# Two weight tiles change places with a weight load, and side copies move behind the first outer products of each block

## The chip, the cores and the metric

The kernel runs on one core of one Trainium2 chip. The metric is device time in microseconds (us). Three executions of the kernel before took 599.28, 599.32 and 602.76 us; their median is 599.32 us. The profile is of another execution of the same kernel, which took 597.99 us; the span from its first to its last instruction is 596.2 us.

## What is computed

The reference is one decode step of a transformer block with conditioned layer norms, forward and backward in one launch:

```python
mod = (silu(c) @ w_mod).reshape(1, 6, 1, 1024)
sa, ca, ga, sb, cb, gb = mod[:, 0], ..., mod[:, 5]
h = layernorm(x) * (1 + ca) + sa
x = x + ga * attention(h, k_cache, v_cache, wq, wo)   # window of the last 4096 of 65536 keys
h = layernorm(x) * (1 + cb) + sb
x = x + gb * (((sigmoid(h @ w_gate)) * (h @ w_up)) @ w_down)
out, vjp = jax.vjp(f, x, k_cache, v_cache, wq, wo, w_gate, w_up, w_down, c, w_mod)
return out, *vjp(grad_out)
```

There is one token of width 1024, 32 query heads on 4 key heads of 128, and a hidden width of 3584. The outputs are the token and the gradients of all ten inputs. Each weight gradient is an outer product as large as the weight. The gradients of the two caches are zero outside the window, and these zeros (some 118 MB) have to be written as well.

## The kernel before, in words

One big tile in on-chip memory, `arena`, holds nearly everything. `ar(off, size)` cuts `size` KiB per partition from it at `off`, and the kernel reuses the same place for many things one after the other. The order of the instructions on each engine is written out by hand. Loads and stores are issued from two queues: POOL's (`nc.gpsimd`) carries most of them and all zero fills, SP's (`nc.sync`) carries the w_down traffic and some tiles of w_mod. Each queue issues in the order of the program: what waits at its head holds up all that stands behind it.

The zero fills are 1 MB writes which `zero(n)` takes from a list, some at each of many places (`Z_B`, `Z_FOLD`, `Z_FFN` and others hold how many).

The stretch around the change has two parts.

**The handover (about 284 to 312 us).** The attention part leaves eight tiles B_t[0] to B_t[7]. `bch` (L682) computes them in chunks on PE, and the last eight chunks, those of tile 7, run between the steps of `fold_half` (L871), which adds three sections of w_mod on PE and copies them back with ACT. The operands of the chunks of tile 7 stand in `ar(56, 8)`: two chunks are done with each 2 KiB of it, so places 56, 58, 60 and 62 come free in turn. The tiles `g_t` (L495) of the last section of w_mod are loaded into such places by `wm_sec` (L337). `mod_gb` (L610) reads them on PE and makes the vector gb, from which the broadcast row `b1k` is made (L933). B_t[4] and B_t[6] stand at 156 and 158, inside the second half of the w_down buffer `wd_v` (L846, places 152 to 160). So `load_wd(0, 1)` may be issued only when B_t[4] has been copied to `scr` and B_t[6] transposed by `tr_unit` (L833) into another home. `tr_unit` is eight PE transposes into one PSUM tile and one ACT copy out of it. After `rot[:] = [(psum, "mm")]` (L804) its PSUM tile, those of `fold_half` and those of `bcast` are one and the same bank.

**The block loop (about 320 to 475 us).** The hidden width is cut in seven blocks of 512. For block q the loop over j = 0 to 7 (L1022) runs on the tiles of w_up and w_gate (`ug_v`, two blocks' worth): DVE reduces the tile with the row `dug_b` (L1024), then the same place is overwritten by an outer product, the gradient, by ACT for j = 0 to 4 and by DVE for 5 to 7 (L1027). `store_ug` (L867) stores tiles 0 to 3 after j = 3 and the others after j = 7, `load_ug` (L863) refills the places for block q + 2. The next block then needs, in this order: `wd_ttr(q+1, 0)` on DVE (L977), `front` on PE (L948), `gates` on ACT (L959), `hh_ops` on DVE, `ffn_mm` on PE, `wd_ttr(q+1, 1)`, `dug_part` (PE and ACT, L986), and `wd_outer` (L981), which overwrites the w_down tile by its gradient and stores it on SP; `load_wd` for the block after waits for that store.

Beside this work runs a list of 45 side jobs (`jobs`, L935 and L996), each of them one `tr_unit`: transposes of tiles which the last part of the kernel needs. `side(n)` (L445) runs the next n of them at that place of the order. Their PSUM bank is also that of `dug_part`.

After the loop comes the last part: the gradients of the attention weights, the caches and w_mod, nearly all of it outer products and stores.

Of the kernel before, what the change touches and what calls it, by code (L numbers as in the profile page):

```python
# [58 lines left out]
def kernel(  # L59
# [26 lines left out]
    nc = tc.nc  # L86
# [13 lines left out]
    def ar(off, size):  # L100
        return arena[:, int(off * KIB):int((off + size) * KIB)]
# [51 lines left out]
    def zero(n, after=None):  # L153
        for _ in range(n):
            if len(zleft) <= keep[0]:
                return
            region, narrow_ = zleft.pop(0)
            first = None
            if narrow_:
                nc.gpsimd.inc_swdge_sem([], [], mode="reset_dge_cursor")  # L160
                n = nlen - ncount.pop()
                first = nc.gpsimd.dma_start(
                    out=rest[0:NS, 0:nlen * 128].rearrange("p (t x) -> p t x", t=2)[:, :, n * 64:(n + 1) * 64],
                    in_=zeros[0:NS, 0:64].rearrange("p (t x) -> p t x", t=1).broadcast_to([NS, 2, 64]))
                ins = nc.gpsimd.dma_start(
                    out=region[8:P, :].bitcast(FP32).rearrange("(t p) x -> p t x", t=2),
                    in_=zeros[0:60, :].rearrange("p (t x) -> p t x", t=1).broadcast_to([60, 2, ZW // 2]))
            else:
                ins = nc.gpsimd.dma_start(out=region.bitcast(FP32), in_=zeros[:, :])  # L169
            if after is not None:  # L170
                dep(first or ins, after)
# [16 lines left out]
    def new_tp(name="tp"):  # L188
        p, tag = next_pool()
        return p.tile([P, 1024], BF16, name=name, tag=tag)  # L190
# [7 lines left out]
    def addv(out, a, b):  # L198
        return tt(out, a, b, ALU.add)

    def cp(out, a):
        return nc.vector.tensor_copy(out=out, in_=a)  # L202
# [6 lines left out]
    def ttr(out, w, b, acc):  # L209
        return nc.vector.tensor_tensor_reduce(out=out, in0=w, in1=b, scale=1.0, scalar=0.0,  # L210
                                              op0=ALU.mult, op1=ALU.add, accum_out=acc)
# [117 lines left out]
    B_t = [junk if o is None else ar(o, 2) for o in B_off]  # L329
# [7 lines left out]
    def wm_sec(sct, j, n, off, eng=nc.gpsimd):  # L337
        eng.dma_start(out=ar(off, 2 * n).rearrange("p (j x) -> p j x", j=n),
                            in_=wm_view[:, j:j + n, sct * D:(sct + 1) * D])

    def mod_tiles(ps, tiles, ts_, first, last=KD - 1):
        for t in ts_:
            for k in range(KD):
                nc.tensor.matmul(ps[:, k:k + 1], lhsT=tiles[t][:, k * P:(k + 1) * P],
                                 rhs=cs_bf[:, t:t + 1], start=(first and t == ts_[0] and k == 0), stop=(t == last),
                                 skip_group_check=True)
# [98 lines left out]
    def side(n=1):  # L445
        for _ in range(n):
            if jobs:
                jobs.pop(0)()
# [35 lines left out]
    for ch in range(8):  # L484
# [7 lines left out]
        if ch % 2:  # L492
            wqT_unit(KD - 1, ch // 2, "AV"[ch // 2 % 2])
        zero(Z_KC[ch], mm)
    g_t = [ar(o, 2) for o in (48, 50, 52, 54, 58, 60, 160, 162)]  # L495
    wm_sec(5, 6, 2, 160)
    load_wo(2)
    load_wo(1)
# [183 lines left out]
    def bch(n=1):  # L682
        for _ in range(n):
            if not bq:
                return
            p, i, u = bq.pop(0)
            if i == 0:
                bbank[p] = bank_pair("b_ps", p)
            for a in range(4):
                h = 4 * u + a  # L690
                for k in range(2):
                    mm = nc.tensor.matmul(bbank[p][k][:, :], lhsT=a4[:, p, h, :], rhs=wo_t[u][:, a, k * 512:(k + 1) * 512],  # L692
                                          start=(i == 0 and a == 0), stop=(i == 7 and a == 3))
            zero(Z_B[nbq - 1 - len(bq)], recent(mm, 3))
            if i == 7:
                for k in range(2):
                    o = B_t[p][:, k * 512:(k + 1) * 512]
                    if k == 0 or p == NBP - 1:
                        nc.scalar.copy(out=o, in_=bbank[p][k][:, :])
                    else:  # L700
                        cp(o, bbank[p][k][:, :])
# [131 lines left out]
    def tr_unit(blk, dst=None):  # L833
        def run():
            tp = new_tp("tp_side")
            for i in range(8):
                nc.tensor.transpose(tp[:, i * P:(i + 1) * P], blk[:, i * P:(i + 1) * P], ident_bf[:, :])  # L837
            nc.scalar.copy(out=blk if dst is None else dst, in_=tp[:, :])  # L838
        return run
# [8 lines left out]
    def wd_dram(t, q, s):  # L848
        return t[q * FB + s * 256:q * FB + s * 256 + 256, :].rearrange("(p j) d -> p j d", j=2)

    def load_wd(q, s):
        nc.sync.dma_start(out=wd_v[:, 2 * s:2 * s + 2, :], in_=wd_dram(B_w_down, q, s))
# [14 lines left out]
    def store_ug(q, j0, n):  # L867
        for k, view in ((0, dwu_view), (1, dwg_view)):
            nc.gpsimd.dma_start(out=ug_part(view, q, j0, n), in_=ug_tile(q, k, j0, n))  # L869

    def fold_half(t, k):  # L871
        ps = new_ps("fold_ps")
        for i in range(4):
            nb = 4 * k + i
            for x, src in enumerate((ga_t[t], cb_t[t], sb_t[t])):
                nc.tensor.matmul(ps[:, i * P:(i + 1) * P], lhsT=src[:, nb * P:(nb + 1) * P], rhs=ident_bf[:, :],
                                 start=(i == 0 and x == 0), stop=(x == 2), skip_group_check=True)
        nc.scalar.copy(out=w2_t[t][:, k * 512:(k + 1) * 512], in_=ps[:, :])
# [16 lines left out]
    park(3, pna, "na")  # L895
    load_wd(0, 0)
    bch(2)
    tr_unit(B_t[6], ar(56, 2))()
    cp(scr, B_t[4])
    B_t[4] = scr  # L900
    load_wd(0, 1)
    mod_tiles(md_ps, sb_t, range(4, 8), False)
    cp(sb_, md_ps[:, 0:KD])
    mulv(h2, ln2, cb1)
# [4 lines left out]
    bch(1)  # L909
    fold_half(4, 1)  # L910
    bch(1)
    wm_sec(5, 4, 1, 58, nc.sync)
    fold_half(5, 0)
    bch(1)
    fold_half(5, 1)
    fold_half(6, 0)
    bch(1)
    wm_sec(5, 5, 1, 60, nc.sync)
    fold_half(6, 1)
    bch(1)  # L920
    fold_half(7, 0)
# [37 lines left out]
    def gates(q):  # L959
        r, gu = small[q % 2], gu_t[q % 2]  # L960
        nc.scalar.activation(out=r["sg"], in_=gu[:, 0:4], func=ACT.Sigmoid)
        nc.scalar.activation(out=r["om"], in_=gu[:, 0:4], func=ACT.Sigmoid, scale=-1.0)
# [14 lines left out]
    def wd_ttr(q, s):  # L977
        for i in (2 * s, 2 * s + 1):
            ttr(junk, wd_v[:, i, :], b1k, small[q % 2]["dhh"][:, i:i + 1])

    def wd_outer(q, s):  # L981
        for i in (2 * s, 2 * s + 1):
            outer_dve(wd_v[:, i, :], small[q % 2]["hh"][:, i:i + 1], b1k)
        store_wd(q, s)
# [11 lines left out]
    jobs.append(tr_unit(B_t[7]))  # L996
    for h in range(HQ):
        jobs.append(tr_unit(wo_t[h // 4][:, h % 4, :]))
    B_home = [ar(o, 2) for o in (24, 26, 28, 30, 40, 42, 56, 62)]

    def unpark(p):
        nc.scalar.copy(out=B_home[p], in_=BT_ps[p][:, :])
# [9 lines left out]
    dug_part(0)  # L1012
    wd_outer(0, 0)
    wd_outer(0, 1)
    side(2)
    zero(Z_FOLD[2])
    load_wd(1, 0)
    load_wd(1, 1)
    for q in range(NB):
        z = Z_FFN[q]  # L1020
        more = q + 1 < NB
        for j in range(KD):  # L1022
            w = ug_v[:, q % 2, j // 4, j % 4, :, :].rearrange("p k f -> p (k f)")
            ttr(w, w, dug_b, dh2acc[:, q * KD + j:q * KD + j + 1])  # L1024
            if not more and j in (3, 5, 6):
                unpark({3: 2, 5: 0, 6: 4}[j])
            (outer_act if j < 5 else outer_dve)(w, h2[:, j:j + 1], dug_b)  # L1027
            if more and 0 < j < 5:
                side()
            if j == 0:  # L1030
                if q == 0:
                    cp(ffn, ffn_ps)
                else:
                    addv(ffn, ffn, ffn_ps)
            if j == 3:
                store_ug(q, 0, 4)
                zero(z[0])
        store_ug(q, 4, 4)
        zero(z[1])
        if more:  # L1040
            wd_ttr(q + 1, 0)
            side(2)
            front(q + 1)
            gates(q + 1)
            hh_ops(q + 1)
            ffn_mm(q + 1, 0)
            ffn_mm(q + 1, 1)
            wd_ttr(q + 1, 1)
            dug_part(q + 1)
            if q + 2 < NB:  # L1050
                load_ug(q + 2, 0, 4)
            wd_outer(q + 1, 0)
            wd_outer(q + 1, 1)
            zero(z[2])
            side()
            if q + 2 < NB:
                load_ug(q + 2, 4, 4)
            zero(z[3])
            if q + 2 < NB:
                load_wd(q + 2, 0)  # L1060
                load_wd(q + 2, 1)
        else:
            zero(z[2] + z[3])
# [5 lines left out]
    B_t = B_home  # L1069
# [264 lines left out]
```

## Time and profile before

| what | value |
|---|---|
| median of three executions | 599.32 us |
| profiled execution | 597.99 us |
| its span | 596.2 us |
| bytes moved by DMA | 246.63 MB, mean 414 GB/s |
| PE busy | 412.4 us (69%) |
| DVE busy | 337.7 us (57%) |
| ACT busy | 264.6 us (44%) |
| POOL busy | 160.6 us (27%) |
| handover and start of block 0, 300 to 320 us | 404 GB/s, TensorE clock 0.80 |
| block loop, 318 to 480 us | 410 GB/s, TensorE clock 0.50 |
| w_down loads, issue to landing | 9.4 to 11.5 us, median 10.0 |

The busy times overlap, since the engines run side by side. A page line such as "DVE junk L210 <- DMA arena<-in_B_w_down_dram: 32.0, 6, 7.8" in the view of waits names the waiting engine with what it writes and its line, then what ended the wait, then the total in us, how often, and the longest. A line of the timeline gives start and duration in us, engine, line, operation, what it writes from what, the shape, how many were merged, and in brackets the idle time before it and what ended that. "DMA share" in the windows view is the packets' time over the time of the 16 DMA engines; it can pass 1.00 because packets of one engine overlap.

### The profile page before, as it was taken

To read this page: it belongs to the slowest core of one execution; us is meant where nothing else is said; L and a number is where in the kernel's file an instruction comes from. 1 tells how busy PE (TensorE), PEld (TensorE's weight loads), DVE (VectorE), ACT (ScalarE), POOL (GpSimd) and SP (SyncE) were. 2 spreads that over 40 slices of the span, in tenths; PEclk is the share of its full clock that TensorE was granted. 3 is DMA by queue.
4 is the path that set the end of the run, shared out by engine and by line. 5 is a ranking of instruction groups with operands and counts; after the bars stand their busy time and mean duration, and the time that the engine had idled before them with its cause. 6 is when DMAs were issued, how large, how long until landed. Compare 5 with 4: busy or idle time off the path is not lost. (4 is left out here: it accounts for less than half of the span.)

```text
span 596.2 us, 11062 instructions
## 1 busy us (share of the span) xinstructions
PE 412.4 (69%) x4612; PEld 278.2 (47%) x4612; DVE 337.7 (57%) x641; ACT 264.6 (44%) x408; POOL 160.6 (27%) x253
## 2 busy tenths in 40 slices
PE   3997688999999989989984444444445184697220
PEld 3996333334344545546654433434334163586220
DVE  3654498999511010070119495797786985698260
ACT  2489514567211014212234572754745733786110
POOL 3113123222223113222221342423423163233100
PEclk9999699999999999999995555555555586755555
DMA  8999999999999999999999999999999999999997
GB/s 349 419 418 421 411 428 411 427 424 425 428 419 423 423 429 423 420 425 423 423 396 411 420 414 408 391 404 415 408 403 416 420 422 414 421 421 423 425 426 319
DMA packets 45026, 246.63 MB, mean 414 GB/s; under 512 B 5085, under 2 KB 5085, under 8 KB 24544
## 3 DMA queue, kind: packets, MB, share of 16 engines
q0 software_dynamic: 37536, 217.60, 95.1%
q1 hardware_dynamic: 7392, 28.32, 12.4%
q8 instruction: 36, 0.59, 0.4%
q14 instruction: 14, 0.11, 0.1%
q10 hardware_dynamic: 48, 0.01, 0.0%
HBM read 60.30 MB, written 185.60 MB: 412 GB/s over the span
## 5 line engine op out<-in xcount | busy, mean ns | idle before, releaser
L692 PE MATMUL b_ps<-arena 128*128 128x512 bf16 x512 | 116.2, 379 | 0.0
L169 POOL DMA_DIRECT2D out_dram<-zeros x114 | 62.8, 553 | 172.0 <-PE n_ps L637 45.5
L837 PE MATMUL tp_side<-ident_bf,arena 128*128 128x128 bf16 x432 | 51.7, 299 | 54.7 <-ACT arena L838 45.9
L193 DVE TENSOR_TENSOR arena<-arena 128x2048 bf16<-128x2048 bf16 x64 | 76.5, 1223 | 2.3 <-PE n_ps L637 0.3
L692 PEld LDWEIGHTS <-arena 128*128 128x128 bf16 x512 | 48.7, 98 | 55.9 <-issue 2.9
L837 PEld LDWEIGHTS <-arena 128*128 128x128 bf16 x432 | 44.2, 140 | 62.3 <-issue 62.0
L838 ACT COPY arena<-tp_side 128x1024 bf16<-128x1024 bf16 x54 | 54.0, 1013 | 41.8 <-PE tp_side L837 40.9
L637 PE MATMUL n_ps<-arena 128*128 128x512 bf16 x256 | 65.8, 378 | 6.2 <-DVE arena L193 4.6
L210 DVE CUSTOM_DVE_ANT_0 arena<-arena,scr 128x1024 bf16<-128x1024 bf16 x56 | 66.2, 1221 | 3.5 <-ACT scr L993 3.5
L210 DVE CUSTOM_DVE_ANT_0 junk<-arena,b1k 128x1024 bf16<-128x1024 bf16 x28 | 34.3, 1224 | 32.6 <-DMA arena<-in_B_w_down_dram 32.0
L637 PEld LDWEIGHTS <-arena 128*128 128x128 bf16 x256 | 24.6, 97 | 41.6 <-issue 16.2
L241 ACT ACTIVATE arena<-scr,h 128x1024 bf16<-128x1024 bf16 x35 | 39.3, 1148 | 0.0
L202 DVE CAST arena<-b_ps 128x512 bf16<-128x512 f32 x6 | 4.2, 692 | 61.6 <-PE b_ps L692 61.6
L1159 PE MATMUL ps_kv<-junk,arena 8*128 8x128 bf16 x256 | 27.1, 304 | 14.1 <-DVE arena L206 12.8
L1163 ACT ACTIVATE arena<-ps_kv 128x512 bf16<-128x512 f32 x48 | 26.2, 686 | 24.2 <-PE ps_kv L1159 23.7
L601 ACT CAST arena<-t_ps 128x512 bf16<-128x512 f32 x56 | 30.1, 589 | 12.1 <-PE t_ps L599 12.1
L869 POOL DMA_DIRECT2D out_dram<-arena x28 | 21.3, 766 | 51.5 <-ACT arena L241 44.8
L1159 PEld LDWEIGHTS <-arena 8*128 8x128 bf16 x256 | 25.2, 140 | 15.9 <-issue 15.8
L993 ACT COPY scr<-tp_dug 128x1024 bf16<-128x1024 bf16 x7 | 7.1, 1012 | 41.4 <-issue 41.4
L456 ACT COPY arena<-tp_wq 128x1024 bf16<-128x1024 bf16 x23 | 21.8, 1034 | 8.1 <-PE tp_wq L454 8.1
L865 POOL DMA_DIRECT2D arena<-in_B_w_up_dram x14 | 10.5, 753 | 48.3 <-DMA out_dram<-arena 26.2
L206 DVE TENSOR_SCALAR arena<-arena,cs_col 128x4096 bf16<-128x4096 bf16 (+1 forms) x16 | 16.0, 1017 | 10.5 <-DMA out_dram<-arena 10.5
(302 smaller groups left out, 646.9 us busy)
## 6 DMA issues: line engine op xcount, KB each, us to landing
out_dram<-zeros POOLq DMA_DIRECT2D x114, 1024.0 KB, 15.3
out_dram<-arena POOLq DMA_DIRECT2D x27, 1024.0 KB, 17.0
out_dram<-arena POOLq DMA_DIRECT2D x30, 512.0 KB, 11.3
out_dram<-arena SPq DMA_DIRECT2D x20, 512.0 KB, 10.7
arena<-in_A_wq_dram POOLq DMA_DIRECT2D x8, 1024.0 KB, 20.7
arena<-in_A_wo_dram POOLq DMA_DIRECT2D x8, 1024.0 KB, 12.0
arena<-in_w_mod_dram POOLq DMA_DIRECT2D x7, 1024.0 KB, 18.1
arena<-in_B_w_down_dram SPq DMA_DIRECT2D x14, 512.0 KB, 10.0
```

The source lines that it names most:

```text
L169: ins = nc.gpsimd.dma_start(out=region.bitcast(FP32), in_=zeros[:, :])
L193: return nc.vector.tensor_tensor(out=out, in0=a, in1=b, op=op)
L210: return nc.vector.tensor_tensor_reduce(out=out, in0=w, in1=b, scale=1.0, scalar=0.0, op0=ALU.mult, op1=ALU.add, accum_out=acc)
L241: return nc.scalar.activation(out=out, in_=b, func=ACT.Copy, scale=col)
L456: nc.scalar.copy(out=blk, in_=tp[:, :])
L601: nc.scalar.copy(out=o, in_=ps)
L637: mm = nc.tensor.matmul(nbank[k][:, :], lhsT=k_nat[:, g, t_ * DH:(t_ + 1) * DH], rhs=vp[:, t_ % 2, 4 * k:4 * k + 4, :].rearrange("p h d -> ...
L692: mm = nc.tensor.matmul(bbank[p][k][:, :], lhsT=a4[:, p, h, :], rhs=wo_t[u][:, a, k * 512:(k + 1) * 512], start=(i == 0 and a == 0), stop= ...
L837: nc.tensor.transpose(tp[:, i * P:(i + 1) * P], blk[:, i * P:(i + 1) * P], ident_bf[:, :])
L838: nc.scalar.copy(out=blk if dst is None else dst, in_=tp[:, :])
L1159: nc.tensor.matmul(ps[:, t4 * DH:(t4 + 1) * DH], lhsT=rows[32 * g:32 * g + HG, t_ * P:(t_ + 1) * P], rhs=hd[32 * g:32 * g + HG, :], start= ...
L1163: nc.scalar.activation(out=o, in_=ps[:, :], func=ACT.Copy, scale=float(scale))
```

## The change

It has two parts.

In the handover, the last two tiles of the gb section, `g_t[4]` and `g_t[5]`, get the places 56 and 58 instead of 58 and 60, and their loads on SP are issued two chunks earlier each: the first right after the first two chunks of tile 7, ahead of `load_wd(0, 1)`. B_t[6] gets the home 60 instead of 56, so its `tr_unit` moves behind the sixth chunk, and `load_wd(0, 1)` moves with it, behind both w_mod loads on SP's queue.

In the block loop, the side jobs beside the outer products stand after j = 3 to 6 instead of j = 1 to 4. The two side jobs ahead of block 0's loop are gone, and one more runs ahead of `front` in the blocks q = 0 and q = 1. The number of side jobs is the same.

```diff
-    g_t = [ar(o, 2) for o in (48, 50, 52, 54, 58, 60, 160, 162)]
+    g_t = [ar(o, 2) for o in (48, 50, 52, 54, 56, 58, 160, 162)]
...
     load_wd(0, 0)
     bch(2)
-    tr_unit(B_t[6], ar(56, 2))()
+    wm_sec(5, 4, 1, 56, nc.sync)
     cp(scr, B_t[4])
     B_t[4] = scr
-    load_wd(0, 1)
     mod_tiles(md_ps, sb_t, range(4, 8), False)
...
     fold_half(4, 1)
     bch(1)
-    wm_sec(5, 4, 1, 58, nc.sync)
+    wm_sec(5, 5, 1, 58, nc.sync)
     fold_half(5, 0)
     bch(1)
     fold_half(5, 1)
     fold_half(6, 0)
     bch(1)
-    wm_sec(5, 5, 1, 60, nc.sync)
+    tr_unit(B_t[6], ar(60, 2))()
+    load_wd(0, 1)
     fold_half(6, 1)
...
-    B_home = [ar(o, 2) for o in (24, 26, 28, 30, 40, 42, 56, 62)]
+    B_home = [ar(o, 2) for o in (24, 26, 28, 30, 40, 42, 60, 62)]
...
     wd_outer(0, 0)
     wd_outer(0, 1)
-    side(2)
     zero(Z_FOLD[2])
...
             (outer_act if j < 5 else outer_dve)(w, h2[:, j:j + 1], dug_b)
-            if more and 0 < j < 5:
+            if more and 2 < j < 7:
                 side()
...
         if more:
             wd_ttr(q + 1, 0)
-            side(2)
+            side(3 if q < 2 else 2)
             front(q + 1)
```

## The prediction

> **What bounds the kernel now.** I read the page first (slices, then the chain of waits), then the windows view in 5 us stretches, then the waits, and last the timeline of the two places that the diff touches.
>
> ```profile
> DMA  8999999999999999999999999999999999999997
> GB/s 349 419 418 421 411 428 411 427 424 425 428 419 423 423 429 423 420 425 423 423 396 411 420 414 408 391 404 415 408 403 416 420 422 414 421 421 423 425 426 319
> DMA packets 45026, 246.63 MB, mean 414 GB/s; under 512 B 5085, under 2 KB 5085, under 8 KB 24544
> ```
>
> Every slice but the first and last has the 16 DMA engines busy 90% or more, while PE, DVE and ACT are below that for most of the second half. The windows view agrees: in none of the 5 us stretches from 5 to 590 us is the DMA share under 1.00. 246.63 MB at the mean of 414 GB/s is 595.7 us, the span of 596.2 us less half a microsecond. So this is a kernel that moves a fixed number of bytes. The slow slices are not idle ones: 300 to 320 us runs at 404 GB/s with a share of 1.09, and the whole block loop (318 to 480 us) at 410 GB/s with 1.08. They carry more of the smaller packets[...]. At the other end nothing computes after 577 us, yet 575 to 590 us moves 423 GB/s: some 15 us of stores stand in the queues when the last instruction is done, so a compute engine that ends later has that much cover.
>
> ```profile
> POOL out_dram L869 <- ACT arena L241: 44.8, 7, 11.9
> ...
> DVE junk L210 <- DMA arena<-in_B_w_down_dram: 32.0, 6, 7.8
> ...
> PE g_ps L344 <- DMA arena<-in_w_mod_dram: 0.7, 1, 0.7
> ...
> DVE hh_bf L193 <- ACT om L962: 0.4, 1, 0.4
> ```
>
> These are the waits from 280 to 480 us. POOL waits for the outer products before it may store, DVE waits for w_down, PE waits only 0.7 us for the last w_mod tile. The gates are waited for once, 0.4 us.
>
> **What the Trainium skill says.** "DMA: Bandwidth & Descriptors", section "Issuing engines are not separate DMA queues", says that transfers of SP and POOL run on the same 16 engines and interleave; the trace agrees, since in the block loop both have transfers under way and the sum stays at 410 GB/s. Its section "Where 436 GB/s comes from" puts the ceiling at 435 GB/s; the best slice here is 429. So 2 to 5% is all that a perfect mix could give. "Perfetto Trace Analysis", section "Per-instruction lifecycle: what the profiler-reported window actually captures", says that a DMA's movement lies outside its instruction's window; hence I use issue to landing: w_down loads take 9.4 to 11.5 us here, though 0.52 MB at 411 GB/s is 1.3 us. Nearly all of a landing is standing in line.
>
> **The change part by part.** Durations are of the profiled execution (597.99 us, of which the span is 596.2).
>
> *Same bytes.* No DMA is added, removed or resized, and the counts of zero fills are the same. Effect on the bound: 0.
>
> *Handover, 285 to 312 us.*
>
> ```profile
> 288.79 0.61 PE L837 MATMUL tp_side<-ident_bf,arena 128*128 128x128 bf16 x8
> ...
> 289.44 1.01 ACT L838 COPY arena<-tp_side 128x1024 bf16<-128x1024 bf16 x1 [5.01 <-PE tp_side L837]
> ...
> 290.50 0.83 PE L876 MATMUL fold_ps<-ident_bf,arena 128*128 128x128 bf16 x12 [0.32 <-ACT arena L838]
> ...
> 309.32 0.35 PE L344 MATMUL g_ps<-cs_bf,arena 128*128 128x1 bf16 x8 [0.68 <-DMA arena<-in_w_mod_dram]
> ```
>
> Taking tr_unit(B_t[6]) out at 289 us gives back 0.65 us of transposes and the 0.32 us in which the fold waited for its copy: -1.0. Put back ahead of fold_half(6,1), now at 301.59, it costs 0.65 plus about 1.05 for the copy, because both write the one "mm" bank and the fold waits: +1.7. On ACT that copy leaves an idle stretch of 5.01 us and now stands between two fold copies; its 1.05 us is the one just counted. The w_mod tiles: SP issued them at 295.49 and 301.78; now they go at about 289 and 295, some 6.3 us earlier, landing (7.5 us) by 304, so the 0.7 us wait goes: -0.7. Sum 0.0: the gb product still ends near 309.7. load_wd(0,1) moves past both on SP, from 289.5 to about 302; at the w_down worst landing of 11.5 it is there by 313.5. Its first reader, wd_ttr(0,1), starts at 315.8, so 2 us are left, and nothing stands behind it on SP until the store at 319.3. If that cover were gone, each us late would go straight into the first block.
>
> *Block loop, 320 to 475 us.* A side unit is 1.01 us of transposes (half clock), then 1.01 us of ACT copy, about 2.1 us from one to the next, since they share one bank. Between outer products the transposes hide under an ACT product of 1.1 us; outside they are exposed. Before, four ride between the products (after j = 1 to 4) and two follow. After, those at j = 3 and 4 ride free, those at j = 5 and 6 follow the last ACT product. So two more exposed transposes, 2 x 1.1 = +2.2 us, before front(q+1), and another +2.1 us where q = 1 has a third unit ahead of front. For q = 0 the two units at 320.64 and 322.75 go: counted from the end of the dug copy (320.58), the five products and the first two copies then end at about 9.0 us, five exposed units at 19.5 and the gates at 20.4, against 18.7 now (339.26), +1.7. The fourth block shows what that meets:
>
> ```profile
> 409.25 1.89 PE L955 MATMUL fg<-h_bf,arena 128*128 128x1 bf16 x64
> ...
> 410.30 1.23 DVE L210 CUSTOM_DVE_ANT_0 junk<-arena,b1k 128x1024 bf16<-128x1024 bf16 x1 [4.25 <-DMA arena<-in_B_w_down_dram]
> 411.18 0.17 ACT L961 ACTIVATE sg<-fg 128x4 f32<-128x4 f32 x1 [0.67 <-PE fg L955]
> 411.25 0.17 ACT L962 ACTIVATE om<-fg 128x4 f32<-128x4 f32 x1
> ...
> 412.72 0.15 DVE L193 TENSOR_TENSOR hh_bf<-sg,fg 128x4 bf16<-128x4 f32 x1
> ```
>
> The gates end at 411.42 and DVE asks for them at 412.72: slack 1.3 us, against +2.2, so hh is 0.9 us late. The same subtraction in the other blocks, gates' end to hh: 363.46 to 366.95 (3.5 against 4.3: 0.8 late), 388.73 to 389.65 (0.9: 1.3 late), 434.49 to 436.54 (2.05: 0.15 late), 458.31 to 460.06 (1.75: 0.45 late); in the first, 339.26 to 341.69 (2.4 against 1.7: none). Together 3.6 us of DVE waiting for ACT. What is late next: w_down's outer products, their store on SP, and the next w_down load.
>
> Against it, store_ug(q,0,4) is released by the product of j = 3, which now has no side copies ahead of it: about 2 us earlier in five blocks, and in the first at about 326.8 instead of 331.24, 4.4 us. The second pair needs DVE's j = 7 product, which doesn't move (1.3 us earlier in the first block, where ACT's j = 4 was last).
>
> What of this reaches the end? A w_down store takes 6.3 to 9.0 us and the load after it 9.9 to 11.5 (the chain of waits), 16 to 20 us a block of which 2.6 us is moving bytes. If the store is issued 0.9 us later, the engines have meanwhile moved 0.9 us more of what stood before it, and it lands when it would have. I take 0 of the 3.6 us, and bound it by 0 and 3.6. The earlier stores only stand in line sooner: I take 0, bounded by -3.8, the block loop at 420 instead of 410 GB/s (162 x 10/420 = 3.9, nearly).
>
> *Rest.* The new homes of g_t and B_home change no instruction. Sum: 0.0 us, a span of 596.2 and 597.99 profiled. The median shown, 599.32, is 1.3 us above that execution, and the forecast for it is **599.3 us**.
>
> **Rivals.**
>
> *Late gates are not absorbed (slower).* For: DVE's wait for w_down is on the chain in all six blocks, and slice 26 (391 GB/s) shows a line that is already short there. Against: the share stays 1.02 even from 370 to 380 us. Price: +3.6, 602.9 us. At worst no w_down wait covers any of it: 1.7 + 4.3 + 4 x 2.2 = 14.8 us, 614 us. It passes 1% from 6.0 us, 1.2 us a block in five blocks, so only when the w_down landings come earlier by that much as well and the engines run dry.
>
> *Earlier stores fill the line (faster).* For: POOL waits 44.8 us for the products, the largest wait that the diff touches. Against: the engines aren't idle in these waits. Price: up to -3.8, 595.5 us.
>
> *The second half of w_down is late.* For: it is issued 12 us later. Against: 2 us of slack at the worst landing, more at the median of 10.0. Price 0 to +2, 600 to 601 us.
>
> *The w_mod loads don't come earlier in effect.* They wait for PE's chunks of the last B tile in any case and the gb product is placed after the last fold; then the handover is +0.7, 600.0 us.
>
> **How the numbers follow.** The forecast (DMA bound, 598 to 601 us) has 0.68, the second half late or w_mod unhelped 0.08, late gates in part or whole up to 605.3 us 0.09 and beyond that 0.05, earlier stores down to 593.4 us 0.08 and beyond 0.02. The three runs before spread by 3.5 us, so I set 596.5 to 602.5 us for 8 in 10. About 1% (6.0 us) is what a measurement of this kernel can tell from no change: faster 0.02, within 0.93, slower 0.05.
>
> **What would show it.** Right: GB/s of the block loop within 405 to 415; POOL's wait on the products down from 44.8 to some 30 us; DVE waiting for the gates for about 3 to 4 us in all, and for w_down for less than 32.0 by a like amount; g_ps without its 0.7 us wait; some 15 us of stores after the last compute. Wrong: a stretch with a DMA share under 0.95 between 320 and 480 us, block starts that drift apart by over 1 us each, or a w_down wait ahead of wd_ttr(0,1).

## The result and the profile after

The change made the kernel slower by about 1%: 606.36 us (median of 6 executions, 605.37 to 609.28) against 600.28 us before (median of 6, 599.28 to 602.76). The ratio is 1.0105, with a 95% interval of 1.0073 to 1.0138, so slower is certain and "by over 1%" is not. The forecast of 599.3 us was wrong, and its range of 596.5 to 602.5 us did not hold the time. The profiled execution took 606.07 us with a span of 604.3 us, each 8.1 us more than before (597.99 us and 596.2 us). In the experiments below the ratios leave out executions that ran more than 1.5% above their kernel's fastest, and the medians keep them.

The page of the kernel after, its DMA lines over 40 slices of 15.1 us:

```profile
DMA  8999999999999999999999999999999999999997
GB/s 350 419 418 418 413 425 419 425 425 427 425 423 423 425 425 422 427 423 423 420 402 409 416 393 382 402 370 406 376 359 418 400 407 411 419 420 423 425 425 290
DMA packets 45026, 246.63 MB, mean 408 GB/s; under 512 B 5085, under 2 KB 5085, under 8 KB 24544
```

The count of packets and the bytes are the same, and outside the block loop the rates are nearly so (just behind it, slices 32 and 33 have 400 and 407 instead of 420 and 422). Slices 24 to 30 (347 to 453 us) are those that fell: 393, 382, 402, 370, 406, 376 and 359 where the same slices of before had 414, 408, 391, 404, 415, 408 and 403. Yet the line above them still says 9 everywhere: the digit that the forecast leaned on doesn't see the loss.

The waits of the kernel after from 280 to 480 us (total, times, longest, in us):

```profile
POOL out_dram L869 <- ACT arena L241: 39.7, 6, 7.1
...
DVE junk L210 <- DMA arena<-in_B_w_down_dram: 25.4, 9, 9.5
...
POOL out_dram L869 <- ACT arena L838: 15.7, 6, 3.0
DVE hh_bf L193 <- ACT om L962: 15.1, 5, 4.1
```

DVE now waits 15.1 us for the gates, where before it was 0.4, and 25.4 us for w_down instead of 32.0. The wait of g_ps for w_mod (0.7 us) is gone from the list.

The windows of the kernel after show where the bytes were missing. The columns are busy time of PE, its weight loads, DVE, ACT and POOL with instruction counts, the granted TensorE clock, DMA share and GB/s.

```profile
318.00:480.00 162.00, 68.23 (x994) 59.80 (x991) 117.20 (x244) 87.90 (x97) 48.84 (x69) 0.50 1.10 395
...
395.00:405.00 10.00, 4.05 (x56) 3.51 (x57) 9.58 (x23) 4.00 (x6) 3.03 (x4) 0.50 0.99 344
445.00:450.00 5.00, 1.62 (x24) 1.38 (x25) 4.50 (x10) 0.87 (x1) 2.68 (x4) 0.50 0.82 273
480.00:485.00 5.00, 0.00 (x0) 0.00 (x0) 4.89 (x10) 5.00 (x7) 2.08 (x3) 0.50 0.85 314
```

This window, which holds the loop, runs at 395 GB/s instead of 410. Over 162 us that is 2.4 MB not moved, 5.9 us at 410 GB/s: nearly the whole loss. The granted clock is not the reason; it is 0.50 there in both kernels. Between 5 and 590 us only the last two of these, 5 us each, have a share under 0.95.

**Block by block.** I measure a block from the end of one copy of the `dug` row (L993 in the kernel after, "scr<-tp_dug" on ACT) to the end of the next one; six such blocks make the loop. The values are worked out from the timelines of the profiled executions, in us. "Gates" is how long after the block's start ACT has finished L962.

| | first block starts | gates | blocks | loop | from loop to end of span |
|---|---|---|---|---|---|
| before | 320.6 | 18.7, then 16.6 | 26.3 25.3 22.7 23.1 23.8 23.5 | 144.7 | 130.9 |
| after | 322.1 | 20.45, 20.75, then 18.64 | 28.5 26.0 24.5 24.2 24.9 23.9 | 151.9 | 130.3 |

The loop is 7.2 us longer, it starts 1.5 us later, and the rest is 0.6 us shorter: together the 8.1 us. The late start isn't the change's: PE is already 1.8 us behind at 285 us, ahead of the first edit, and the medians differ by 6.1 us, not 8. What has to be explained is some 6 us, and the block loop is where the trace has them.

### The profile page after: what moved, and what is told of

Read it like the earlier page. It is cut to its first block, busy times and chain, and to the rows that moved or that the text cites. A ratio compares the mean times of both kernels' runs of the same rounds, so it can differ in the third digit from the quotient of the medians.

```text
span 604.3 us, 11036 instructions
## 1 busy us (share of the span) xinstructions
PE 411.0 (68%) x4586; PEld 279.4 (46%) x4612; DVE 337.2 (56%) x641; ACT 264.9 (44%) x408; POOL 160.6 (27%) x253
## 2 busy tenths in 40 slices
DMA packets 45026, 246.63 MB, mean 408 GB/s; under 512 B 5085, under 2 KB 5085, under 8 KB 24544
## 5 line engine op out<-in xcount | busy, mean ns | idle before, releaser
L837 PEld LDWEIGHTS <-arena 128*128 128x128 bf16 x432 | 44.7, 142 | 76.5 <-issue 76.3
L692 PEld LDWEIGHTS <-arena 128*128 128x128 bf16 x512 | 49.6, 100 | 58.0 <-issue 6.7
L210 DVE CUSTOM_DVE_ANT_0 junk<-arena,b1k 128x1024 bf16<-128x1024 bf16 x28 | 34.3, 1224 | 26.0 <-DMA arena<-in_B_w_down_dram 25.4
L637 PEld LDWEIGHTS <-arena 128*128 128x128 bf16 x256 | 24.6, 97 | 41.6 <-issue 16.2
L1162 ACT ACTIVATE arena<-ps_kv 128x512 bf16<-128x512 f32 x48 | 26.2, 686 | 25.2 <-PE ps_kv L1158 25.0
L601 ACT CAST arena<-t_ps 128x512 bf16<-128x512 f32 x56 | 30.1, 588 | 12.1 <-PE t_ps L599 12.1
L1158 PEld LDWEIGHTS <-arena 8*128 8x128 bf16 x256 | 25.0, 139 | 16.6 <-issue 16.6
L456 ACT COPY arena<-tp_wq 128x1024 bf16<-128x1024 bf16 x23 | 21.8, 1034 | 8.3 <-PE tp_wq L454 8.3
L206 DVE TENSOR_SCALAR arena<-arena,cs_col 128x4096 bf16<-128x4096 bf16 (+1 forms) x16 | 16.0, 1014 | 11.1 <-DMA out_dram<-arena 11.0
L993 ACT COPY scr<-tp_dug 128x1024 bf16<-128x1024 bf16 x7 | 7.1, 1012 | 34.3 <-issue 34.3
L878 ACT CAST arena<-fold_ps 128x512 bf16<-128x512 f32 x16 | 9.4, 586 | 28.3 <-PE fold_ps L876 28.3
## 6 DMA issues: line engine op xcount, KB each, us to landing
out_dram<-zeros POOLq DMA_DIRECT2D x114, 1024.0 KB, 16.6
```

The costliest lines, as they stand in the source:

```text
L206: return nc.vector.tensor_scalar(out=out, in0=a, scalar1=s1, scalar2=None, op0=op0)
L601: nc.scalar.copy(out=o, in_=ps)
L637: mm = nc.tensor.matmul(nbank[k][:, :], lhsT=k_nat[:, g, t_ * DH:(t_ + 1) * DH], rhs=vp[:, t_ % 2, 4 * k:4 * k + 4, :].rearrange("p h d -> ...
L1158: nc.tensor.matmul(ps[:, t4 * DH:(t4 + 1) * DH], lhsT=rows[32 * g:32 * g + HG, t_ * P:(t_ + 1) * P], rhs=hd[32 * g:32 * g + HG, :], start= ...
L1162: nc.scalar.activation(out=o, in_=ps[:, :], func=ACT.Copy, scale=float(scale))
```

## The experiments

The first theory after seeing this was that late gates lengthen each block and that nothing later gives it back. The rivals were the handover (the second half of w_down issued 12 us later), and the earlier gradient stores standing ahead of w_down. Every kernel does all of the work; the time of each is set against that of the kernel before in the same batch (its medians there: 599.7, 599.9 and 599.5 us).

**1. The handover edits alone** (g_t and B_home, the two w_mod loads, B_t[6] and load_wd(0, 1) as in the diff; block loop as before).

> The handover edits alone (new homes, earlier w_mod loads, later tr_unit and load_wd(0, 1)); the block loop and its side jobs as before. Theory (an engine loop of ACT and PE ahead of front is now longer than the DMA work of a block): within 1.5 us of before. Rival 1 (the late second half of w_down starts the block loop late): the whole +6 us. Rival 2 (earlier gradient stores stand ahead of the w_down transfers): within 1.5 us of before, as the theory has it.

Measured: 599.28 us, ratio 0.9983 (0.995 to 1.0015); loop 144.8 us. The handover costs nothing.

**2. The loop edits alone** (the last three hunks of the diff; handover as before).

> The block loop's edits alone (side jobs after j = 3 to 6, none ahead of block 0, three ahead of front in the first two blocks); the handover as before. Theory: the whole loss, +5 to +7 us, blocks about 24 us apart from the third on. Rival 1: within 1.5 us of before. Rival 2: +5 to +7 us.

Measured: 606.86 us, ratio 1.0112 (1.0082 to 1.0141); loop 152.9 us. The whole loss is in these three hunks. The blocks of its trace are 29.0 26.0 24.6 24.3 23.9 25.2.

**3. The change, with the last side jobs behind the gates**

```diff
             wd_ttr(q + 1, 0)
-            side(3 if q < 2 else 2)
             front(q + 1)
             gates(q + 1)
+            side(3 if q < 2 else 2)
             hh_ops(q + 1)
```

> The change, but the two or three side jobs that stand ahead of front in each block stand behind the gates; those beside the outer products stay after j = 3 to 6, so the first gradient store stays as early as in the change. Theory: two exposed side jobs, 4.2 us, leave the engine loop, which falls from 24 to about 20 us and under the 23 us that a block's DMA work takes; the loss goes, within 1.5 us of before. Rival 2: the stores are as early as in the change, so +5 to +7 us stays.

Measured: 600.42 us, ratio 1.0011 (0.9976 to 1.0045). The gates come 14.1 to 14.4 us into a block, and DVE's wait for them is down to one:

```profile
DVE hh_bf L193 <- ACT om L962: 0.4, 1, 0.4
```

The line is of the waits of this kernel from 280 to 480 us. Its first block is even longer than that of the change (30.0 us), and the later ones make up for it (24.3 21.1 24.5 23.7 23.6). Same units, same earlier stores, same handover; only the units' place against `front` differs, and the loss is gone. Gates that come late are what the loss needs.

**4. The change, with all four units behind the products**

```diff
-            if more and 2 < j < 7:
-                side()
+            if more and j == 7:
+                side(4)
```

> The change, but all four side jobs of the loop stand after j = 7. The products and the first store are as in the change; one more transpose is exposed in each of six blocks, 1.1 us each. Theory: 6 x 1.1 = 6 to 7 us above the change, 12 to 13 us above before. Rival 2: as the change, +6 us.

Measured: 609.2 us, ratio 1.0132 (1.0079 to 1.0185); blocks 30.5 27.0 24.9 24.9 24.9 24.9, gates at 19.7 us in the last four. The direction is right, and so is the step: the gates came 1.04 us later than in the change, one more exposed transpose, and the last four blocks are gates + 5.24 us to within 0.01 us. The expected total was too large (12 to 13 us above before; the medians differ by 9.5 us, the ratio gives 7.9), because it was added to blocks of the change that were already longer than their gates + 5.24 us.

**5. The moved units alone** (before, without `side(2)` ahead of block 0 and with `side(3 if q < 2 else 2)` ahead of `front`; the four between the products stay at j = 1 to 4).

> Before with one part of the loop's edits: no side jobs ahead of block 0, three instead of two ahead of front in the first two blocks; those beside the outer products stay after j = 1 to 4. Theory: the gates come 16.6 and 18.7 us after the dug copy in the first two blocks, before the hidden unit is asked for at 20 to 21 us, so within 1.5 us of before. Rival (any rearrangement of these side jobs disturbs the queues): slower by some us.

Measured: 599.88 us, ratio 1.0009 (0.9987 to 1.003); loop 145.3 us. Costs nothing. In its trace the gates come after 18.2 us in the first block (16.6 was expected, before has 18.7) and after 18.7 us in the second, the only one in which they come later than before; there w_down still came last.

**6. The shift alone**

```diff
-            if more and 0 < j < 5:
+            if more and 2 < j < 7:
```

> Before with the other part alone: side jobs after j = 3 to 6 instead of j = 1 to 4, all else as before. Theory: the engine loop is 24 us in every block, against 22.7 to 23.6 us from the third block on before, so +3 to +6 us, most of the change's loss. Rival (the third side job ahead of front in the first two blocks is what costs): within 1.5 us of before.

Measured: 602.94 us, ratio 1.0047 (1.0022 to 1.0073); blocks 26.4 27.0 23.9 23.9 23.9 23.9. Four blocks of one length are the sign of a loop that waits for itself. Its timeline at the end of the fifth block:

```profile
438.09 1.89 PE L955 MATMUL fg<-h_bf,arena 128*128 128x1 bf16 x64
...
440.09 0.17 ACT L962 ACTIVATE om<-fg 128x4 f32<-128x4 f32 x1
440.29 0.16 DVE L193 TENSOR_TENSOR hh_bf<-sg,fg 128x4 bf16<-128x4 f32 x1 [3.09 <-ACT om L962]
...
444.49 1.01 ACT L993 COPY scr<-tp_dug 128x1024 bf16<-128x1024 bf16 x1 [4.23 <-issue]
```

From the end of the gates at 440.26 to the end of the copy at 445.50 are 5.24 us without a DMA wait, and the gates ended 18.65 us after the copy before: 18.65 + 5.24 = 23.89.

**7. Before, with its own units behind the gates**

```diff
             wd_ttr(q + 1, 0)
-            side(2)
             front(q + 1)
             gates(q + 1)
+            side(2)
```

> Before, with the two side jobs ahead of front moved behind the gates: its engine loop falls from about 22 to about 18 us. Theory: a block's DMA work of 23 us is the bound there, so nothing is gained, within 1.5 us of before. Rival (the engine loop was a bound before already, so each us taken from it is a gain): 3 us or more faster than before.

Measured: 600.95 us, ratio 1.0014 (0.9998 to 1.0031). The gates come at 12.4 us instead of 16.6 and nothing is gained. Before was not limited by them. The blocks of its trace are 27.1 25.4 24.5 24.1 24.0 21.1.

**8. The change, with three fills moved out of the last part into the loop.** If the loss is an idle line, work for the line must bring it back without making the loop shorter. Three 1 MB zero fills of the last part go behind the second gradient stores of the third to fifth block.

```diff
-Z_FFN = [(1, 1, 0, 2)] + [(1, 0, 0, 2)] * 4 + [(1, 1, 1, 2), (1, 2, 1, 0)]
-Z_END = (1, 2, 1, 0, 0)
+Z_FFN = [(1, 1, 0, 2), (1, 0, 0, 2)] + [(1, 1, 0, 2)] * 3 + [(1, 1, 1, 2), (1, 2, 1, 0)]
+Z_END = (1, 0, 0, 0, 0)
```

> The change with three zero fills moved from the last part of the kernel into the third to fifth block, right after the second pair of gradient stores; nothing else moves, and the engine loop stays as long. Theory: the change loses because the DMA engines have too little in line while the loop waits for its engines; 3 MB more to write there take 7 us of DMA time that was lost, so most of the loss comes back, 600 to 603 us. Rival (the late engine loop costs by itself, through the work that follows it): as the change, 605 to 608 us.

Measured: 601.31 us, ratio 1.0022 (1.0005 to 1.0039). The loop is as long as in experiment 2 (152.8 us, gates at 18.65), but it moves more, in the same window of this kernel:

```profile
318.00:480.00 162.00, 68.15 (x984) 59.74 (x984) 116.69 (x242) 88.68 (x98) 50.42 (x73) 0.50 1.13 408
```

408 GB/s instead of 395 in the change and 394 in experiment 2, and the rest takes 124.4 us instead of 130.3. Some 5 of the 6 us come back while the engines are as late as ever. So the loss is not engine time as such; it is bytes that the queues weren't given in time. What these fills would do in the kernel before was not run.

**9. The change, with the first block's units as before**

```diff
-            if more and 2 < j < 7:
+            if more and (0 < j < 5 if q == 0 else 2 < j < 7):
```

> The change, but in the first block the side jobs stand after j = 1 to 4 as before; from the second block on after j = 3 to 6. The first gradient store of the first block is then issued about 8.0 us after the dug copy instead of 6.25, after the w_down load. Theory with two parts (engine loop of 24 us in the later blocks, and in the first block earlier stores ahead of the w_down load): the first block falls from 28.4 to about 26.6 us, the others stay near 24, so 2 us of the change's 6 come back, 603.5 to 605 us. Engine loop alone: as the change, 606 us.

Measured: 604.49 us, ratio 1.0072 (1.0035 to 1.0109). The median is 1.9 us below the change's, as expected, but the interval holds the change's own ratio of 1.0105, so that the first block costs 2 us is not shown. Its trace (an execution of 608.19 us) has blocks of 26.8 26.5 25.6 23.9 24.8 25.8: the first as expected, the others not near 24 throughout. And the first gradient store went 0.17 us ahead of the w_down load in it, not behind.

**10. Before, with the first block's units as in the change** (no `side(2)` ahead of it, j = 3 to 6 in it alone, and `side(3 if q < 2 else 2)`).

> The reverse: side jobs after j = 3 to 6 in the first block alone, after j = 1 to 4 in the others, none ahead of block 0 and three ahead of front in the first two blocks. Theory: the first block takes 28.5 to 30 us, but the later blocks have an engine loop of 22 us under the 23 us of their DMA work, so the queues stay fed and nothing is lost, within 1.5 us of before. If the first block's delay costs by itself: 2 to 3 us more than before.

Measured: 601.15 us, ratio 1.0024 (1.0004 to 1.0044); blocks 27.7 25.8 24.0 21.8 22.5 24.1. In its trace the first block is 1.4 us longer than before, and the fourth and fifth are shorter: blocks with slack win part of it back.

The profiled executions of experiments 7, 9 and 10 ran 3 to 4 us longer than the medians of their kernels, with a loop that began at 322.4 to 324.0 us; for them the medians and ratios count, not the spans.

## Why the prediction was wrong, point by point

**The step that failed is "I take 0 of the 3.6 us, and bound it by 0 and 3.6".** Its reason was that a w_down store that is issued later lands when it would have, because the line ahead of it has got shorter. The line did get shorter: w_down came sooner after the dug copy than before in four of the five blocks after the first (12.1 to 14.3 us instead of 15.4 to 17.6), and DVE's wait for it fell from 32.0 to 25.4 us. It was of no use. The timeline of the kernel after in its fourth block:

```profile
414.69 1.23 DVE L210 CUSTOM_DVE_ANT_0 junk<-arena,b1k 128x1024 bf16<-128x1024 bf16 x1 [2.68 <-DMA arena<-in_B_w_down_dram]
...
417.57 1.89 PE L955 MATMUL fg<-h_bf,arena 128*128 128x1 bf16 x64
...
419.57 0.17 ACT L962 ACTIVATE om<-fg 128x4 f32<-128x4 f32 x1
419.77 0.16 DVE L193 TENSOR_TENSOR hh_bf<-sg,fg 128x4 bf16<-128x4 f32 x1 [2.58 <-ACT om L962]
```

w_down is there at 414.69, where before it set the pace, and DVE then has nothing to do from 417.19 to 419.77: `front` stands behind the exposed transposes. A wait in a queue can absorb a delay only while it is the last one. From the dug copy through products, exposed units, `front`, gates, hh and dug runs a loop of engine work without any DMA in it. It takes gates + 5.24 us: 21.8 before, 23.9 in the change. The DMA work of a middle block is 9.4 MB (4 loads and 4 stores of w_up and w_gate tiles and 4 of w_down, 0.52 MB each, and 3 fills of 1.05 MB), 23.0 us at 410 GB/s. Roughly, the longer of the two is the block: before that was the transfers, by 1.2 us; in the change it is the engines, by 0.9 us.

The engines' side is shown: in experiments 4 and 6 eight blocks in all are gates + 5.24 us to within 0.01 us. The transfers' side is less sure. 410 GB/s is what the kernel before moved here, so the 23.0 us describe its blocks (22.7 to 23.8) and do not bound them. It may be w_down's round trip that paced them, since its store must land before the next load may go: in the trace of experiment 7, whose engine loop is 17.6 us, the third to fifth blocks took 24.0 to 24.5 us at only 383 to 394 GB/s, with DVE waiting for w_down. Which of the two it was is open.

The experiments agree with this comparison. Taking the ratio times 600 us: where the loop of engine work is below 23 us in the later blocks (experiments 1, 3, 5, 7, 10) the loss is at most 1.4 us; at 23.9 it is 2.8 (6), 4.3 (9), 6.7 (2) and 6.3 us (the change); at 24.9 it is 7.9 (4). Experiment 8 stands apart, since it gave the line other work.

**What failed with it: "a compute engine that ends later has that much cover".** The stores at the end are the last part's own bytes: before computes until 576.7 us and has 19.5 us of stores behind that, the change until 584.7 us and has 19.6. From the loop's end to the end of the span are 130.3 to 131.6 us in eight of the kernels and 132.5 to 133.0 in three (experiments 1, 7, 10), whatever the loop took; only taking 3 MB out of that part shortened it (experiment 8, 124.4). A delay in the loop is passed on whole.

**What lay under both: "the share stays 1.02 even from 370 to 380 us".** It was the reason given against late gates. A share above 1.00 was read as a full line, and the lower rates of the loop were put down to smaller packets. Three windows of the kernel before speak against that:

```profile
325.00:330.00 5.00, 1.93 (x17) 1.60 (x16) 4.93 (x11) 4.95 (x6) 0.00 (x0) 0.50 1.24 424
375.00:380.00 5.00, 1.93 (x18) 1.60 (x16) 4.96 (x10) 4.95 (x6) 0.68 (x2) 0.50 1.01 351
555.00:575.00 20.00, 4.16 (x38) 3.62 (x35) 9.54 (x14) 2.98 (x5) 1.14 (x3) 0.50 1.01 424
```

With mostly packets under 8 KB (397 of 490) the loop could move 424 GB/s, and the share was then 1.24. From 375 to 380 us (449 of 465) it moved 351 at 1.01, the same share with which the last part (536 of 1376) moved 424. That reads as room in the line of the kernel before already, though its packets were smaller still than those of the first window. Two sums of the forecast hid this or show less than they seem to: 246.63 MB at the mean of 414 GB/s gives the span whatever the kernel does, since that mean is the bytes over the span; and the 2 to 5% of room are an estimate from the cited page's 435 GB/s, 1.4% above the best slice and 5.1% above the mean.

**The rival "late gates are not absorbed" was the right mechanism**, and its price of 3.6 us somewhat over half of the 6.1 us that came; its own condition for more, that w_down lands earlier by as much and the engines run dry, is what happened. Taking in each block the longer of before's length and gates + 5.24 gives 26.3 + 26.0 + 4 x 23.9 = 147.9 us, +3.2 on before's 144.7; the shift alone measured +2.8 by its ratio. The change's 151.9 us hold 4.0 more, in two places.

*The first block,* 28.45 instead of 26.3: the rival "earlier stores" with its sign turned. The forecast let stores that are issued 4.4 us sooner "only stand in line sooner". They stand in line ahead of a w_down load. Before, the first block's timeline has the load first:

```profile
327.70 4.54 SPq L852 DMA_DIRECT2D arena<-in_B_w_down_dram  x2
...
331.24 1.52 POOL L869 DMA_DIRECT2D out_dram<-arena  x2 [10.10 <-ACT arena L241]
...
345.62 1.86 SPq L855 DMA_DIRECT2D out_dram<-arena  x2
```

With the loop edits alone (experiment 2) the order is turned:

```profile
326.78 1.64 POOL L869 DMA_DIRECT2D out_dram<-arena  x2 [5.52 <-ACT arena L241]
...
327.64 4.34 SPq L852 DMA_DIRECT2D arena<-in_B_w_down_dram  x2
...
344.67 1.23 DVE L210 CUSTOM_DVE_ANT_0 junk<-arena,b1k 128x1024 bf16<-128x1024 bf16 x1 [1.29 <-DMA arena<-in_B_w_down_dram]
...
348.39 1.13 SPq L855 DMA_DIRECT2D out_dram<-arena  x2
```

The load is issued at the same time and its second half now ends a wait at 344.67 (before, that read began at 342.03, with no wait in the list), so the w_down store follows 2.8 us later. Where the stores came behind the load (experiments 5 and 6, at 328.35 and 329.08 us) the store went at 345.67 and 345.54, as before. The order goes with the first block's length in all twelve kernels: 27.7 to 30.5 us where the stores go 0.7 us or more ahead of the load (the change and experiments 2, 3, 4, 8 and 10), 26.3 to 27.1 us where they go behind (before and experiments 1, 5, 6 and 7), 26.8 in experiment 9. It isn't the gates, for experiment 3 has early gates and 30.0 us. But no run moves the stores alone, and the trace of the change is less clean than that of experiment 2. Like the other three traces with a late loop, it has the load itself issued late, 9.85 us after the dug copy instead of 7.1, because the w_down store before it took 11.1 us instead of 8.4; the load, 3.6 us behind the stores, then took 10.6 us to its first read, not more than the 11.6 of before. How its 2.1 us divide stays open, and so does what they cost at the end.

*Blocks 3 to 5,* 24.5, 24.2 and 24.9 instead of 23.9: one half of w_down comes 0.3 to 1.0 us after the gates would have let DVE go on, and a block that has lost this way has no slack to win it back, as the blocks of experiment 10 have. This, with stores that get ahead of the load only when both parts of the edit are in, would also explain why the parts don't add up: 0 for the moved units, 2.8 for the shift, 6 to 7 for both. Experiment 9 lies 1.5 us above experiment 6 though its first block is as before; the intervals overlap, and I have traced that to no single term.

**What was right.** The handover: its -1.0, +1.7 and -0.7 sum to 0 and experiment 1 finds 0.9983. load_wd(0, 1) went at 302.91 us (about 302 forecast), no w_down wait stands ahead of wd_ttr(0, 1), the wait of g_ps is gone, and the fold waits for the copy in its own bank as said. The kernel after:

```profile
302.23 0.61 PE L837 MATMUL tp_side<-ident_bf,arena 128*128 128x128 bf16 x8
...
302.88 1.01 ACT L838 COPY arena<-tp_side 128x1024 bf16<-128x1024 bf16 x1 [1.59 <-PE tp_side L837]
302.91 0.33 SPq L852 DMA_DIRECT2D arena<-in_B_w_down_dram  x1
303.94 0.83 PE L876 MATMUL fold_ps<-ident_bf,arena 128*128 128x128 bf16 x12 [1.10 <-ACT arena L838]
```

The working in the loop was right too, unit by unit: gates at 20.4 us in the first block (measured 20.45), 20.9 in the second (20.75), 18.8 after that (18.64). The error lay in what the numbers were held against. Lateness was reckoned from when w_down happened to land before, in single blocks (0, 0.8, 1.3, 0.9, 0.15, 0.45), when the question was whether 23.9 us is more than the queues need for a block.

**The signs.** "Block starts that drift apart by over 1 us each" came true in four of six blocks (2.1, 0.7, 1.8, 1.1, 1.1 and 0.4 us longer). "A share under 0.95" came true only for 5 us at 445, while the rate forecast to stay within 405 to 415 GB/s fell to 395. DVE's wait for the gates of 3 to 4 us became 15.1, since in four blocks w_down was there long before the gates. POOL's wait on the first stores fell from 44.8 to 39.7, not to 30: they were released 2 us earlier in a block that was over 1 us longer, and the second pair's wait stands in the list with 15.7 us under a side copy of ACT.

No version beats both kernels beyond the measurement; the handover alone (0.9983) and before are the same.

## What to carry to other kernels

In a loop that runs beside busy queues, work out two lengths of one turn: that of the longest closed chain of engine work with no transfer in it, and that of the turn as its transfers now set it. Added engine work is free while the first stays below the second and is paid in every turn from there (here 21.8 us of chain stood in turns of some 23 us, and 23.9 us was paid); waiting for a transfer elsewhere in the turn didn't absorb it. A store that is made ready sooner may not be free either, if it gets ahead of a load that someone waits for. And a DMA share above 1.00 doesn't say that there is no room.

## What the runs showed of the hardware

The DMA share did not show that the queues ran short. From 370 to 380 us it is 1.02 at 367 GB/s in the kernel after (1.02 at 369 before), from 395 to 405 us 0.99 at 344, though well fed slices have 420 to 427 GB/s; a drop of a fifth in the bytes moved costs a tenth of the share (1.10 over the loop). What share goes with a full line differs, too: 424 GB/s stood at 1.24 in the loop and at 1.01 in the last part of the kernel before. Only gaps as large as 273 GB/s bring it to 0.82. The moved bytes per window, set against what the kernel moves elsewhere, are the number to read.

Two 0.52 MB stores that POOL issued 0.9 us ahead of a w_down load on SP (experiment 2) came with later halves of that load: DVE's first reads moved from 339.27 to 340.54 and from 342.03 to 344.67, by 1.3 and 2.6 us. At 410 GB/s the 1.05 MB of stores are 2.6 us (an estimate), so here an order that differs by 4.4 us of issue in another queue went with a load that was later by up to all the bytes that got ahead. It isn't so each time: in experiment 10 the load went 3.8 us behind the stores and was read 10.0 us after its issue, sooner than the 11.6 us of before. "DMA: Bandwidth & Descriptors", section "Issuing engines are not separate DMA queues", says that the transfers of all issuing engines run on the same 16 engines and interleave; the traces agree, since stores of POOL and a load of SP were under way together in each of these cases.
